# A two-dimensional spectral filter on one core: three quarters of stage 1's constants loaded without their zeros, its matmuls writing every fourth place of PSUM

## The chip, the cores and the metric

The kernel runs on one core of a Trainium2 chip. The metric is the time of one execution on the device in microseconds (us), as a median of several runs. A core has five engines with instruction streams of their own: TensorE (PE, matmuls; PEld is its weight load), VectorE (DVE), ScalarE (ACT), GpSimd (POOL) and SyncE (SP, which here only issues transfers). They meet through semaphores. Matmuls read SBUF and write PSUM, which has eight banks of 512 fp32 per partition.

## The reference

```python
def _A_ref(x, w_r, w_i):
    B, S, D = x.shape
    X = jnp.fft.rfft2(x.astype(jnp.float32), axes=(-2, -1))
    W = w_r + 1j * w_i
    X = X * W
    y = jnp.fft.irfft2(X, s=(S, D), axes=(-2, -1)).astype(jnp.bfloat16)
    return y
...
x = A_x
g = _sigmoid((x * gate_w).sum(-1, keepdims=True))
a = _A_ref(x, A_w_r, A_w_i)
b = _B_ref(x, B_w_r, B_w_i)      # the same filter with other weights
return g * a + (1 - g) * b
```

x is 1 x 2048 x 1024 in bf16, and each weight is 2048 x 513 (real and imaginary part, for A and B). So one picture is transformed, its spectrum is multiplied with two complex masks, both products are transformed back, and a gate per row mixes the two.

## The kernel before

All transforms are matmuls with constant matrices, and a 2048-point transform is split in two steps of 32 and 64 points. Stage 1 does the 32-point step over the rows, stage 2 the transform over the columns, stage 4 the 64-point step. Then VectorE multiplies with the masks (`product`, L508), and stages 5 to 7 go back: `group` (L604 matmuls, L615 copies), `stage6` (L754) and `stage7` (L783 matmuls, L790 and L794 results).

Each engine runs its instructions in the order in which the program adds them; `Prog` puts waits where a key that one instruction reads or writes was touched by another. A DMA is in the stream of the engine that issues it and can hold up what stands behind it there.

Stage 1 works on four blocks of rows, c = 0 to 3. A block holds four residues r = 4c + q, and a partition is n1 * 4 + b, with n1 of 32 and b of 4. For a block:

- SP loads x (nine loads for the four blocks, 4 MB in all), and VectorE folds it into `XF` (`fold`, L340), twice over, as sums and as differences (h).
- The constants of stage 1 are in the tile `MM`: four blocks of 512 columns, one block for each c, and behind them, from column 2048, the same negated (`negate`, L359 on ScalarE for blocks 0 and 1, L357 on VectorE for 2 and 3). Column r * 128 + t * 8 + ri * 4 + b' of `MM` belongs to residue r, frequency t, real or imaginary part ri, and row class b'. On partition n1 * 4 + b it is other than zero only where b' = b: three quarters of `MM` are zeros.
- 32 matmuls (L379) have 128 x 128 of `XF` as weights and stream 256 columns: 128 of `MM` twice, once as they are and once negated (or twice as they are). Two matmuls add up in one stretch of 256 fp32 of PSUM. Eight of them fill two banks (a slot u of four), and one copy of 1024 elements per partition (L390 on ScalarE, L388 on VectorE for two of the sixteen) takes them to `FT`.

The order of the matmuls is block by block; inside a block by h, then by the half j, then by residue q. A matmul waits for its fold, for its constants and for their negation.

The constants come in three loads: block 0 from ScalarE's queue, ahead of its table load, its sigmoid and its negation; block 1 from SP behind the three x loads of block 0; blocks 2 and 3 in one load from SP behind the two x loads of block 1. SP goes on with the rest of x, the constants of stage 2 (`F2`), the gate's weights (`GR`), `CK`, `SM` and then the 44 loads of the masks into `W` (`wload`), which VectorE's products wait for. VectorE's stream begins with the folds of blocks 0 and 1. `fold3` (L438) and `stage2` (L451, L460) follow stage 1 and read `FT`.

Outputs of matmuls in the other stages lie in PSUM in runs of 32 and more, with two small exceptions: `star_column` (L527) writes 15 columns to every second place, and some matmuls of two columns write 32 places apart. `col0` (L582) reads its moving operand from `W` with a step of one row of 520 elements, or from `XF` side by side.

Of the kernel before, what the change touches and what calls it, by code (L numbers as in the profile page):

```python
# [17 lines left out]
def bf16_bits(a):  # L18
    a = np.ascontiguousarray(np.asarray(a, dtype=np.float32))
    u = a.view(np.uint32).astype(np.uint64)  # L20
    r = ((u + 0x7FFF + ((u >> 16) & 1)) >> 16).astype(np.uint16)
    return r


def make_consts():
    C = {}
    pi2 = 2 * np.pi
    n1 = np.arange(32)
    M = np.zeros((32, 4, 16, 16, 2, 4))
    V = np.zeros((2, 4, 16, 32, 16))  # L30
    for b in range(4):
        for r in range(16):
            n2 = 16 * b + r
            for t in range(16):
# [5 lines left out]
                else:  # L40
# [2 lines left out]
                    M[:, b, r, t, 1, b] = -np.sin(ph)  # L43
                    V[0, b, r, :, t] = np.cos(ph) / 16
                    V[1, b, r, :, t] = -np.sin(ph) / 16
    C["M"] = M.reshape(128, 2048)
    VR = 0.25 * V.reshape(128, 512)
    row = np.arange(128)
    MK = np.zeros((128, 16, 4))
# [4 lines left out]
    for cmb, par in ((0, 0), (1, 1), (2, 1), (3, 0)):  # L54
# [5 lines left out]
        else:  # L60
            F = F[0].reshape(128, 2, 2, 32, 2)
            e = [np.stack([F[:, :, 0, :, w], F[:, :, 1, :, 1 - w]], axis=2).reshape(128, 128) for w in range(2)]
# [28 lines left out]
    c, s = np.cos(pi2 * kk * o2 / 64), np.sin(pi2 * kk * o2 / 64)  # L91
# [4 lines left out]
    e = np.eye(64)  # L96
# [12 lines left out]
    sl_, f = row % 32, row // 32 % 2  # L109
# [14 lines left out]
    for pi in range(2):  # L124
        for h in range(2):
# [5 lines left out]
            a = pi2 * l * (d + 0.5) / 1024  # L131
# [100 lines left out]

def bass_gated_mix__spectral_gfnet__spectral_gfnet__prompt_kernel(nc, A_x, A_w_r, A_w_i, B_x, B_w_r, B_w_i, gate_w, out):
    C = make_consts()
    SMv = C.pop("SM")
    cst = {k: nc.inline_tensor(bf16_bits(v), name=f"c_{k}") for k, v in C.items()}
    cst_sm = nc.inline_tensor(np.ascontiguousarray(SMv, dtype=np.float32), name="c_SM")
    f32, u16 = dt.float32, dt.uint16
# [5 lines left out]
    MM = sb("MM", 7168)  # L244
# [13 lines left out]
    def sl(t, off, dims, p0=0, np_=128, pstep=1):  # L258
        n = t.shape[1]
        return AP(t, p0 * n + off, [[n * pstep, np_]] + [list(x) for x in dims])  # L260

    def ps(col, dims):
        return AP(PS, col, [[4096, 128]] + [list(x) for x in dims])

    def bank(b):
        return ("ps", b)
# [9 lines left out]
    P = Prog()  # L276
# [5 lines left out]
    def dma(eng, name, dst, src, **kw):  # L282
        return P.add(eng, lambda e: e.dma_start(dst, src), dma=name, **kw)  # L283

    def load(name, tile, off, n, src, eng="sp", **kw):
        dma(eng, name, sl(tile, off, [(1, n)]).bitcast(u16), src, **kw)


    def xloc(c):
        return W, (96 + 8 * c) * RP  # L290
# [4 lines left out]
    for _ in range(18):  # L295
        P.add("pe", lambda e: e.matmul(ps(7 * 512, [(1, 256)]), sl(CL, GRo, [(1, 128)]), sl(CL, GRo, [(1, 256)]), start=True, stop=True),
              r=["GRz"], w=[bank(7)])
    def mload(eng, c0, n):
        load(f"M{c0}", MM, c0 * 512, n * 512, cst["M"].ap()[:, c0 * 512:(c0 + n) * 512], eng=eng, w=[("M", c) for c in range(c0, c0 + n)])

    mload("act", 0, 1)
    for c in range(4):
        t, o = xloc(c)
        for q0, n in XPARTS[c]:
            dma("sp", f"x{c}{q0}", sl(t, o + q0 * 1024, [(1, n * 1024)]), xv[:, (4 * c + q0) * 1024:(4 * c + q0 + n) * 1024], w=[("x", c, q0)])
        if c < 2:
            mload("sp", 1 + c, 1 + c)
    load("F2", F2, 0, 1536, cst["F2"].ap(), w=["F2"])
    dma("sp", "GR", sl(CL, GRo, [(1, 128)], np_=8), AP(gate_w.tensor, gate_w.offset, [[128, 8], [1, 128]]), w=["GRz"], a=["GR"])
    load("CK", CK, 0, 1056, cst["CK"].ap(), w=["CK", "GW2"])  # L310
# [40 lines left out]
            fold(c, q0, n, h)  # L351

    def negate(c, n=1, eng="act"):
        dst, src = sl(MM, 2048 + c * 512, [(1, n * 512)]), sl(MM, c * 512, [(1, n * 512)])
        kw = dict(r=[("M", k) for k in range(c, c + n)], w=[("NM", k) for k in range(c, c + n)])
        if eng == "dve":
            P.add("dve", lambda e: e.tensor_scalar(out=dst, in0=src, scalar1=-1.0, scalar2=None, op0=ALU.mult), **kw)  # L357
        else:
            P.add("act", lambda e: e.activation(dst, src, ACT.Copy, scale=-1.0), **kw)  # L359
# [3 lines left out]
    def stage1(c):  # L363
        nonlocal cnt
        us = [(cnt + k) % 4 for k in range(4)]
        cnt += 4
        parts = XPARTS[c] if c == 0 else ((0, 4),)
        for q0, n in parts:
            for h in range(2):
                for j in range(2):  # L370
                    u = us[2 * h + j]
                    for q in range(q0, q0 + n):
                        r = 4 * c + q
                        base = (c % 2) * 4096 + q * 1024 + h * 512
                        o = ps(u * 1024 + q * 256, [(1, 256)])
                        for s in range(2):
                            lh = sl(XF, base + 256 * s + 128 * j, [(1, 128)])
                            rh = sl(MM, r * 128, [(2048 * s, 2), (1, 128)])
                            P.add("pe", lambda e, o=o, lh=lh, rh=rh, s=s: e.matmul(o, lh, rh, start=(s == 0), stop=(s == 1)),  # L379
                                  r=[("xf", c % 2, q, h, s ^ j), ("M", c), ("NM", c)], w=[bank(2 * u + q // 2)])  # L380
                    if q0 + n < 4:
                        continue
                    for m0, mn in ((0, 32), (32, 96)) if (c, h, j) == (3, 1, 1) else ((0, 128),):
                        src = ps(u * 1024 + m0, [(128, 2), (1, mn), (256, 4)])
                        dst = sl(FT, h * 8192 + j * 2048 + 16 * m0 + 4 * c, [(4096, 2), (16, mn), (1, 4)])
                        kw = dict(r=[bank(2 * u), bank(2 * u + 1)], a=[("F1", h, j)] + [("F1a", h, j)] * (m0 == 0))
                        if (c, h, j) in ((2, 1, 1), (3, 0, 1)):
                            P.add("dve", lambda e, s=src, d=dst: e.tensor_copy(d, s), **kw)  # L388
                        else:
                            P.add("act", lambda e, s=src, d=dst: e.activation(d, s, ACT.Copy), **kw)  # L390

    negate(0)
    negate(1)
    folds(0)
    folds(1)
    negate(2, 2, "dve")
    stage1(0)
    stage1(1)
    fold(2, 0, 2, 0)
    fold(2, 2, 2, 0)  # L400
    fold(2, 0, 4, 1)
    folds(3)
    stage1(2)
    stage1(3)

# [276 lines left out]
    def spare():  # L682
        slots.append(slots.pop(0))
        return slots[-1]
# [33 lines left out]
    u = spare()  # L718
# [207 lines left out]
```

## Time and profile before

| | |
|---|---|
| median of 3 runs | 118.17 us (118.08 to 118.53) |
| profiled execution | 118.88 us, span 116.6 us |
| PE, PEld busy | 110.0 us (94%), 88.4 us (76%) |
| DVE, ACT, POOL busy | 100.7 us (86%), 96.5 us (83%), 34.0 us (29%) |
| granted TensorE clock | 0.991 |
| DMA | 26.14 MB, 17682 packets, mean 224 GB/s |
| stage-1 matmuls (L379) | 128, 14.9 us, 273 ns each |
| their weight loads | 128, 12.2 us, 98 ns each |
| copies L390 | 15, 13.1 us, 1012 ns each |
| folds L340 | 34, 11.4 us, 5.9 us idle before them |
| first load of M, on ACT | 128 KB, 3.7 us from issue to landing |

Times are those of one profiled execution; starts count from its span's start, and about 2.3 us of the execution lie around the span. The time of an instruction reaches from its start to its end; matmuls overlap, so that the distance from one start to the next (the pitch) is shorter than the time of one. A group's line has its busy time, the mean of one in ns, and the idle time of its engine just before.

### The profile page before, as it was taken

What the parts mean: (1) busy time and instruction counts of PE and PEld (TensorE: products, weight loads), DVE (VectorE), ACT (ScalarE), POOL (GpSimd) and SP (SyncE); (2) the same over time, 40 slices, a digit from 0 to 9 for tenths busy, and PEclk for the clock granted to TensorE, in tenths of its full rate; (3) what the DMA queues carried; (4) which work ended last, traced back from release to release, by engine and by line L of the source; (5) the groups of instructions that cost most, each with busy time, mean ns of one, the idle gap of its engine ahead of it and who ended that gap; (6) DMA issues with size and microseconds to landing.
All of it is one profiled execution on the core that took longest, in us unless ns stands there. A gap on an engine that the chain in (4) does not pass through costs nothing.

```text
span 116.6 us, 4237 instructions
## 1 busy us (share of the span) xinstructions
PE 110.0 (94%) x1812; PEld 88.4 (76%) x1812; DVE 100.7 (86%) x210; ACT 96.5 (83%) x117; POOL 34.0 (29%) x43
## 2 busy tenths in 40 slices
PE   6999999999999999999999999999999999999950
PEld 4666888875766657569999999999988777777430
DVE  0478998978999999699999999999568999899990
ACT  5239998997799999939999999997879889988420
POOL 1000030016655600000000000000002999999930
PEclk9999999999999999999999999999999999999996
DMA  3999999999999999962369930000000135425466
GB/s 86 289 405 415 421 359 355 352 349 350 363 370 358 368 364 362 350 241 100 139 172 407 389 123 0 6 0 6 0 6 0 46 146 181 181 96 193 153 233 236
DMA packets 17682, 26.14 MB, mean 224 GB/s; under 512 B 2112, under 2 KB 11072, under 8 KB 17664
## 3 DMA queue, kind: packets, MB, share of 16 engines
q1 hardware_dynamic: 16368, 23.00, 56.2%
q0 software_dynamic: 864, 2.36, 5.6%
q10 hardware_dynamic: 432, 0.52, 1.4%
q8 instruction: 14, 0.23, 0.8%
q14 instruction: 4, 0.03, 0.1%
HBM read 17.48 MB, written 4.19 MB: 186 GB/s over the span
## 4 chain that ended last, share of the span: by engine, by line
PE 51%; SPq 29%; DMA 9%; DVE 3%; issue 2%; ACT 2%; DVEq 0%
SPq L283 29%; PE PS L604 26%; PE PS L783 15%; PE PS L754 7%; DMA W<-in_B_w_i_dram 6%; DMA W<-in_A_x_dram 3%; PE PS L379 2%; DVE W L508 1%; DVE MM L794 1%; ACT W L615 1%; PE PS L563 1%; ACT XF L790 1%; PE PS L582 1%; DVE XF L340 0%; DVEq L865 0%
## 5 line engine op out<-in xcount | busy, mean ns | idle before, releaser
L604 PE MATMUL PS<-CL,W 128*128 128x128 bf16 x512 | 32.3, 225 | 0.2 <-DVE W L508 0.2
L604 PEld LDWEIGHTS PS<-CL,W 128*128 128x128 bf16 x512 | 31.6, 145 | 0.9 <-DVE W L508 0.7
L835 POOL TENSOR_TENSOR MM<-FT 128x512 bf16<-128x512 f32 x14 | 17.4, 1273 | 48.7 <-DVE FT L830 48.7
L615 ACT ACTIVATE W<-PS 128x1024 bf16<-128x1024 f32 (+1 forms) x30 | 28.5, 1036 | 3.0 <-PE PS L604 2.9
L508 DVE TENSOR_TENSOR W<-XF,W 128x1024 bf16<-128x1024 bf16 (+1 forms) x38 | 22.4, 608 | 1.6 <-DMA W<-in_B_w_i_dram 0.9
L508 DVE TENSOR_TENSOR W<-MM,W 128x1024 bf16<-128x1024 bf16 (+1 forms) x38 | 22.4, 613 | 0.2
L783 PE MATMUL PS<-FT,W 128*128 128x256 bf16 (+1 forms) x132 | 19.4, 299 | 0.1
L487 ACT ACTIVATE XF<-PS 128x1024 bf16<-128x1024 f32 x16 | 17.3, 1079 | 1.6 <-PE PS L480 1.6
L480 PE MATMUL PS<-XF,CK 128*128 128x512 bf16 (+1 forms) x72 | 17.8, 357 | 0.1
L767 ACT ACTIVATE W<-PS 128x1024 bf16<-128x1024 f32 (+1 forms) x15 | 14.8, 992 | 2.7 <-PE PS L754 2.7
L340 DVE TENSOR_TENSOR XF<-W 128x512 bf16<-128x512 bf16 (+2 forms) x34 | 11.4, 404 | 5.9 <-DMA W<-in_A_x_dram 5.7
L783 PEld LDWEIGHTS PS<-FT,W 128*128 128x128 bf16 x132 | 12.1, 98 | 5.4 <-DVE XF L794 0.7
L379 PE MATMUL PS<-MM,XF 128*128 128x256 bf16 x128 | 14.9, 273 | 0.6 <-DVE XF L340 0.4
L469 ACT ACTIVATE XF<-PS 128x1024 bf16<-128x1024 f32 x14 | 15.0, 1078 | 0.1
L379 PEld LDWEIGHTS PS<-MM,XF 128*128 128x128 bf16 x128 | 12.2, 98 | 3.5 <-DVE XF L340 2.0
L390 ACT ACTIVATE FT<-PS 128x1024 bf16<-128x1024 f32 (+2 forms) x15 | 13.1, 1012 | 0.8 <-PE PS L379 0.8
L283 POOL DMA_DIRECT2D MM<-XF x18 | 9.9, 550 | 13.4 <-PE PS L480 8.0
L830 DVE TENSOR_TENSOR FT<-PS,XF 128x512 f32<-128x512 f32 x18 | 11.6, 684 | 0.8 <-ACT XF L790 0.4
L451 PEld LDWEIGHTS PS<-F,FT 128*128 128x128 bf16 x128 | 8.4, 98 | 3.1 <-ACT FT L390 0.2
L790 ACT ACTIVATE XF<-PS 128x512 f32<-128x512 f32 (+1 forms) x16 | 8.5, 533 | 2.2 <-PE PS L783 2.2
L451 PE MATMUL PS<-F,FT 128*128 128x128 bf16 x128 | 10.2, 219 | 0.0
L480 PEld LDWEIGHTS PS<-XF,CK 128*128 128x128 bf16 x72 | 4.7, 97 | 6.1 <-ACT XF L487 5.7
(62 smaller groups left out, 104.3 us busy)
## 6 DMA issues: line engine op xcount, KB each, us to landing
W<-in_A_x_dram SPq DMA_DIRECT2D x7, 512.0 KB, 7.5
out_dram<-MM SPq DMA_DIRECT2D x10, 256.0 KB, 2.5
MM<-XF POOLq DMA_DIRECT2D x18, 128.0 KB, 5.4
FT<-c_U SPq DMA_DIRECT2D x1, 2048.0 KB, 8.5
MM<-XF SPq DMA_DIRECT2D x14, 128.0 KB, 2.7
W<-in_A_w_r_dram SPq DMA_DIRECT2D x4, 256.5 KB, 6.3
W<-in_A_w_i_dram SPq DMA_DIRECT2D x4, 256.5 KB, 6.7
W<-in_B_w_r_dram SPq DMA_DIRECT2D x4, 256.5 KB, 7.1
```

What stands on the lines that cost most here:

```text
L283: return P.add(eng, lambda e: e.dma_start(dst, src), dma=name, **kw)
L379: P.add("pe", lambda e, o=o, lh=lh, rh=rh, s=s: e.matmul(o, lh, rh, start=(s == 0), stop=(s == 1)), r=[("xf", c % 2, q, h, s ^ j), ("M", c ...
L451: P.add("pe", lambda e, o=o, cs=cs, j=j, t=t, rh=rh: e.matmul(o, fblock(1 + cs, j, t), rh, start=(j == 0), stop=(j == 1)), r=[("F1a" if p ...
L469: P.add("act", lambda e: e.activation(dst, src, ACT.Copy), **kw)
L480: P.add("pe", lambda e, o=o, kind=kind, pm=pm, m=m, rh=rh: e.matmul(o, sl(CK, fbo(kind, pm, m), [(1, 128)]), rh, start=(m == 0), stop=(m = ...
L487: P.add("act", lambda e: e.activation(dst, src, ACT.Copy), **kw)
L508: P.add("dve", lambda e: e.tensor_tensor(out=rows((1 - h) * 64 * RP + sw * HW), in0=sl(xt, xo + 128 * h + 64 * h0, [(0, 2), (256, 4 * ni), ...
L604: P.add("pe", lambda e, o=o, l0=l0, ab=ab: e.matmul(o, sl(W, HW * ab + l0, [(RP, 128)]), sl(CL, KIo[ab], [(1, 128)]), start=(ab == 0), sto ...
L615: P.add("act", lambda e: e.activation(dst, src, ACT.Copy), r=b, a=keys)
L767: P.add("act", lambda e, s=src, d=dst: e.activation(d, s, ACT.Copy), **kw)
L783: P.add("pe", lambda e: e.matmul(ps(col, [(1, n * 256)]), lh, rh, start=(k == 0), stop=(k == last)), r=[("Y", r), "DI"] + ["DJ"] * (full o ...
L835: P.add("pool", lambda e, s=s, op=op: e.tensor_tensor(out=ods(s, 0, 2), in0=pv[:, :, 0, :], in1=pv[:, :, 1, :], op=op), r=[("PQ", pk, 0), ...
```

## The change

The constants of block 0 are loaded as before, 128 KB, with their columns in another order: by b' first. Of blocks 1 to 3 only the quarter that isn't zero is kept in memory, 384 columns by 128 rows. VectorE clears columns 512 to 2047 of `MM`, and four loads of 32 rows by 384 columns (24 KB each, 768 bytes a row), two from ScalarE's queue and two from SP's, put the rows of each class b in every fourth partition and in that class's 384 columns. They wait for the clearing and share one semaphore. The negations of blocks 1 to 3 read and write four runs of 128 or 256 columns each. A stage-1 matmul reads its 128 columns of `MM` as four runs of 32, and since PSUM is to hold what it held before, writes column b', k to place 4 k + b'. Counts of matmuls, folds and copies stay, and nothing after stage 1 is touched.

```diff
-    C["M"] = M.reshape(128, 2048)
+    MF = M[:, :, :4].transpose(0, 1, 5, 2, 3, 4).reshape(128, 512)
+    MC = np.stack([M[:, b, 4:, :, :, b] for b in range(4)]).reshape(128, 384)
+    C["M"] = np.concatenate([MF, MC], axis=1)
...
-    def mload(eng, c0, n):
-        load(f"M{c0}", MM, c0 * 512, n * 512, cst["M"].ap()[:, c0 * 512:(c0 + n) * 512], eng=eng, w=[("M", c) for c in range(c0, c0 + n)])
-
-    mload("act", 0, 1)
+    load("M0", MM, 0, 512, cst["M"].ap()[:, :512], eng="act", w=[("M", 0)])
+    MR = [("M", c) for c in range(1, 4)]
+    mz = P.add("dve", lambda e: e.memset(sl(MM, 512, [(1, 1536)]), 0.0), w=MR)
+
+    def mrest(eng, gs):
+        for g in gs:
+            dma(eng, "M1", sl(MM, 512 + 384 * g, [(1, 384)], p0=g, np_=32, pstep=4).bitcast(u16), cst["M"].ap()[32 * g:32 * g + 32, 512:],
+                a=MR, after=[mz])
+
+    mrest("act", (0, 1))
     for c in range(4):
         t, o = xloc(c)
         for q0, n in XPARTS[c]:
             dma("sp", f"x{c}{q0}", sl(t, o + q0 * 1024, [(1, n * 1024)]), xv[:, (4 * c + q0) * 1024:(4 * c + q0 + n) * 1024], w=[("x", c, q0)])
-        if c < 2:
-            mload("sp", 1 + c, 1 + c)
+        if c == 0:
+            mrest("sp", (2, 3))
...
     def negate(c, n=1, eng="act"):
-        dst, src = sl(MM, 2048 + c * 512, [(1, n * 512)]), sl(MM, c * 512, [(1, n * 512)])
+        dst, src = (sl(MM, o + (384 + c * 128 if c else 0), [(384 if c else 128, 4), (1, n * 128)]) for o in (2048, 0))
...
-                        o = ps(u * 1024 + q * 256, [(1, 256)])
+                        o = ps(u * 1024 + q * 256, [(128, 2), (1, 4), (4, 32)])
                         for s in range(2):
                             lh = sl(XF, base + 256 * s + 128 * j, [(1, 128)])
-                            rh = sl(MM, r * 128, [(2048 * s, 2), (1, 128)])
+                            rh = sl(MM, r * 32 + 384 * (c > 0), [(2048 * s, 2), (384 if c else 128, 4), (1, 32)])
```

## The prediction

> **What bounds the kernel now.** I read the page first, then the busy time by stage, then the timeline of TensorE and VectorE, then the waits. The chain of waits on the page is led by "SPq L283 29%", the issuing of loads. I do not take that as the bound of the first stage: the chain's last link in that stretch is a W transfer, and the timeline shows what that link is worth.
>
> ```profile
> 5.20:20.40 15.20, 14.66 (x128) 12.24 (x129) 13.61 (x36) 12.35 (x14) 1.31 (x1) 1.00 1.03 391
> 20.40:49.50 29.10, 28.95 (x443) 19.60 (x441) 26.84 (x56) 27.37 (x33) 9.87 (x18) 1.00 1.07 359
> ```
>
> These are the windows: length, then busy time of PE, weight loads, DVE, ACT and POOL, the granted clock, the DMA share and GB/s. The first is stage 1. All its 128 matmuls lie in it, PE is busy 14.66 of 15.20 us at full clock, and DMA moves 391 GB/s.
>
> ```profile
> 5.24 1.91 PE L379 MATMUL PS<-MM,XF 128*128 128x256 bf16 x16
> 13.80 6.82 PE L379 MATMUL PS<-MM,XF 128*128 128x256 bf16 x61
> 20.46 0.20 PE L516 MATMUL PS<-CK,CL 128*128 128x8 bf16 x2
> 48.18 0.44 DVE L508 TENSOR_TENSOR W<-MM,W 128x512 bf16<-128x512 bf16 x1
> 49.51 0.42 DVE L508 TENSOR_TENSOR W<-XF,W 128x512 bf16<-128x512 bf16 x1 [0.89 <-DMA W<-in_B_w_i_dram]
> ```
>
> In the timeline (start, length, engine) the 61 matmuls take 6.82 us. One lasts 0.273, so the pitch is (6.82 - 0.27)/60 = 0.109 us. From 10.5 us on PE runs without a gap to the end of stage 1 at 20.46. TensorE is the bound there; before it, folds that wait for x cost it gaps of together some 1.3 us (15.22 from start to end, less 128 x 0.109). From 33 to 48.6 us VectorE's products and ScalarE's evacuations (one of L469 or L487 every 0.91 us) run without gaps. The W transfers that head the chain then hold VectorE up for 0.89 us, once. From 53.5 to 85 TensorE is full again (17.47 of 17.5 us, then 14.00 of 14.0). Nearly every later step therefore hangs on the end of stage 1, with 0.89 us of slack in between.
>
> **The change, part by part.** Times are those of the profiled execution, 118.88 us with a span of 116.6, which is 0.71 over the median of 118.17. I add differences to both alike.
>
> *Fewer bytes.* Two loads go, 128 KB and 256 KB on SP. Four of 24 KB come: 288 KB less. At the 391 GB/s of the window that is 0.75 us less transfer. SP loses issues of 0.43 and 0.56 us and gains two; the smallest issues on the page's timeline (2 KB) cost 0.35, so SP is 0.1 to 0.3 us earlier. What this can buy is the 0.89 us that VectorE waits for W, and no more, since it waits for no other W load.
>
> *The clearing of the tile.* One VectorE MEMSET of 768 words, ahead of its first fold at 4.64, before which it is idle. POOL's MEMSET of 256 elements took 0.31, so three times as many come to some 0.9 us, done by 1.7. Bounds: 0.3 to 1.2 (a VectorE copy of 1024 elements), and all of them end before 2.2.
>
> *Two issues on ScalarE, behind that wait.* They stand ahead of its table load (1.28 us), its sigmoid (0.20) and the negation of the first block. M0's issue there took 0.36. So 1.7 + 0.72 + 1.28 + 0.20 = 3.9 us; M0 landed at 4.44 and the negation started at 4.46. The cover is 0.5 us, and what exceeds it would delay the first matmul one to one. I take nothing. Queued behind SP's wait are the x loads of blocks 1 to 3, but SP arrives there at 2.1, after the MEMSET.
>
> *The negations read and write runs of 128.* The folds write runs of 128 too, so I take 0.63 and 0.42 us as they are. M1 lands as late as before at worst (7.2 us), and block 1 begins only after 32 matmuls: no cost, with two us to spare.
>
> *The matmuls.* Same count, 256 columns, same weights. Their moving operand comes in runs of 32. Their output goes to every fourth fp32 of PSUM. The page of before has no such output; the nearest rows, by shape:
>
> ```profile
> L379 PE MATMUL PS<-MM,XF 128*128 128x256 bf16 x128 | 14.9, 273 | 0.6 <-DVE XF L340 0.4
> L527 PE MATMUL PS<-GSB,CK 128*128 128x15 bf16 x2 | 0.2, 176 | 0.0
> L527 PE MATMUL PS<-GSB,CK 128*128 128x1 bf16 x2 | 0.2, 164 | 0.0
> L582 PE MATMUL PS<-XF,CL 128*128 128x64 bf16 x2 | 0.4, 188 | 0.0
> L582 PE MATMUL PS<-XF,CL 128*128 128x60 bf16 x2 | 0.4, 188 | 0.0
> L582 PE MATMUL PS<-W,CL 128*128 128x64 bf16 x2 | 0.6, 276 | 0.0
> ```
>
> The fourth number is ns of one. A contiguous output costs (273 - 188)/(256 - 64) = 0.44 ns per column. L527 writes 15 columns to every second place of PSUM (its output is `[(2, n)]`): (176 - 164)/14 = 0.86 ns per column, twice as much. It also reads its operand at step 2, but L582's 60 columns from XF are read at steps of 2 and -1 and written contiguously, and cost the same 188 ns as 64 contiguous ones. So a small step in the read is free, and I put L527's excess down to the write. The excess is 6 ns on two rows, each rounded to 1 ns: a hint, not a measurement. The runs of 32 in the read I take as free by the same L582 row.
>
> Bounds for a step of four: below, nothing, as ScalarE reads PSUM at a step of 256 (L390, 1023 ns per 1024 elements) as fast as contiguously (L487, 1023), though at under half of TensorE's rate (0.91 us per 1024 elements from copy to copy, against 0.109 per 256). Above, the price of a read with each element far from the next: L582 from W, 276 against 188, is 88/64 = 1.4 ns more per column. I take L527's factor of two, the only row with a stepped PSUM write: a pitch of 2 x 0.109 = 0.218 us.
>
> The Trainium skill, page "PSUM — Partial Sum Buffer", section Specifications (TRN2), says that PSUM is laid out in 8-byte lines and that any non-contiguous pattern slows matmuls significantly. It gives no factor; a step of two fp32 already puts each element in a line of its own, so by that rule L527's price would hold for a step of four. L527 is the only row here that agrees, by its 6 ns.
>
> *The sum.* Stage 1 starts at 5.24 as before and is then bound by TensorE alone: 128 x 0.218 = 27.9 us, an end at 33.1 in place of 20.46, so 12.7 later (the 1.3 us of old gaps are swallowed; without them it would be 14.0). PSUM evacuation has room: eight matmuls now take 1.74 us against 0.91 for the ScalarE copy that follows. The folds of blocks 2 and 3 get more time. Late next are the sums and differences of L438 on VectorE, the second stage and the products, all of them hung on stage 1's end. W lands by 49 us while its last user comes at 61, so the 0.89 us wait goes. 12.7 - 0.9 = **11.8 us**: 130.7 for the profiled execution, 130.0 against the median. Own range of this case 128.5 (a shorter tail of evacuations and swaps that land sooner in a quiet DMA) to 131.5 (0.86 ns per column, no gain at W).
>
> **Rivals.** *Stepped PSUM writes run at full rate* (not slower). Then stage 1's end stays near 20.4, because x for block 1 is still queued behind 96 KB of M and the gap at 10 us remains. The gain is W landing 0.75 us sooner, in place of 0.89 us of waiting: 117.4, or 118.2 if SP's issue rate holds W back rather than bandwidth. It decides as long as the pitch stays under 0.116 (0.9/128 above 0.109). For it: ScalarE's free stepped reads, and that L527's evidence is 6 ns. Against it: that this is still the only row with stepped writes, and it doubles. Chance 0.16, with 0.09 for a gain over 0.6 us and 0.07 within it.
>
> *Each write pays as each scattered read does.* L582 from W: 1.4 ns more per column, 256 columns, 128 matmuls: 45 us, so about 162. For it: step four goes further than step two. Against it: L527's step two already leaves no two elements side by side, and costs 0.43 more. Chance 0.08. The Trainium skill, page "SBUF — State Buffer", section "Door 1: The DMA port swizzle", lets each access to a new 16-byte line pay a penalty in SBUF; L582 from W agrees there with its 88 ns, and no row shows PSUM doing so.
>
> *A part of the penalty hides in the array's pipeline*, leaving a pitch of about 0.150: 128 x 0.041 = 5.2 us, less 1.3 of gaps and 0.9 at W: 121 to 123. Nothing in the page speaks for it but the smallness of the hint. Chance 0.06.
>
> **How the numbers follow.** Forecast 0.70, rivals 0.16, 0.08 and 0.06. The time is the forecast's. The range from 117.4 to 131.5 takes in the full-rate case, the partial case and the forecast, and leaves out the scattered price (0.08) and a tenth of the forecast's own spread. What can be told from no change here is 0.5%, 0.6 us: faster 0.09, same 0.07, slower 0.84.
>
> **What would show it.** Right: the stage-1 matmul lasts some 380 ns where it lasted 273, a run of n of them takes 0.217 to 0.222 us each, ScalarE waits some 0.8 us for TensorE ahead of each stage-1 copy, the first product starts near 37.5 in place of 25.2, VectorE's wait for in_B_w_i is gone, and the stretch after stage 5's start has its old length. Wrong: a row that still says 273 ns and a pitch of 0.109 means the full-rate case; 600 ns and more the scattered price; a first matmul later than 5.4 us means that the clearing or ScalarE's queue was not covered.

## The result, and the profile after

The changed kernel takes 130.44 us (median of 6 runs, 130.38 to 131.09) against 118.47 us for the kernel before (median of 6): a ratio of 1.103, with a 95% interval of 1.100 to 1.106. The profiled execution took 131.09 us with a span of 128.8, and 118.88 with 116.6 before.

The timeline of TensorE in the changed kernel (start, length, engine, line, count; stage 1's matmuls are now L387):

```profile
5.04 28.46 PE L387 MATMUL PS<-MM,XF 128*128 128x256 bf16 x128
33.29 0.24 PE L524 MATMUL PS<-CK,CL 128*128 128x8 bf16 x2
```

One unbroken stretch of 128 matmuls replaces 15.2 us with gaps. What follows it starts at 33.29 in place of 20.46, 12.83 us later. The groups by shape (busy time, mean ns of one, then the idle time before them and what ended it) and the busy time by stage (PE, weight loads, DVE, ACT, POOL, clock, DMA share, GB/s):

```profile
L387 PE MATMUL PS<-MM,XF 128*128 128x256 bf16 x128 | 28.5, 428 | 0.0
L387 PEld LDWEIGHTS PS<-MM,XF 128*128 128x128 bf16 x128 | 17.9, 141 | 10.4 <-issue 0.6 <-DVE XF L348 0.4
L398 ACT ACTIVATE FT<-PS 128x1024 bf16<-128x1024 f32 x13 | 13.0, 1025 | 11.4 <-PE PS L387 11.4
```

```profile
5.20:20.40 15.20, 15.20 (x69) 9.64 (x68) 10.85 (x31) 8.15 (x9) 0.53 (x1) 1.00 1.01 374
20.40:33.20 12.80, 12.80 (x61) 8.27 (x60) 3.43 (x7) 5.46 (x6) 0.00 (x0) 1.00 1.10 349
33.20:61.50 28.30, 28.15 (x430) 19.12 (x428) 26.17 (x53) 26.23 (x31) 9.88 (x18) 1.00 0.66 220
```

In the first 15.2 us only 69 matmuls fit where 128 did, and ScalarE, which began 13 copies in that window, begins 8; through stage 1 it waits 11.4 us for TensorE. The third window is the second stage and the products. They take as long as before and are only moved: from the first matmul behind stage 1 to the first of stage 5 (L612, at 63.56 us; 50.80 before) it is 30.27 us, where it was 30.34. The DMA share fell from 1.07 to 0.66, since the last piece of W now lands at 43.9 us (49.4 before), well inside this window. VectorE's wait for W is gone; in the waits from 32 us on, no transfer is listed. The chain of waits says the same in one line each, which in the page of before began with "SPq 29%":

```profile
PE 92%; ACT 3%; DVE 1%; issue 0%; DVEq 0%; POOL 0%; POOLq 0%
PE PS L612 24%; PE PS L387 22%; PE PS L791 13%; PE PS L488 11%; PE PS L762 7%; PE PS L459 5%; PE PS L298 3%; PE PS L468 3%; PE PS L530 2%; ACT XF L495 2%; DVE MM L802 1%; PE PS L571 1%; ACT XF L477 1%; ACT XF L798 1%; PE PS L590 1%
```

### The profile page after: what moved, and what is told of

It is laid out like the page before. It is cut to its first block, busy times and chain, and to the rows that moved or that the text cites. A ratio compares the mean times of both kernels' runs of the same rounds, so it can differ in the third digit from the quotient of the medians.

```text
span 128.8 us, 4241 instructions
## 1 busy us (share of the span) xinstructions
PE 123.0 (96%) x1812; PEld 94.2 (73%) x1812; DVE 101.8 (79%) x211; ACT 97.3 (76%) x117; POOL 33.2 (26%) x43
## 4 chain that ended last, share of the span: by engine, by line
PE 92%; ACT 3%; DVE 1%; issue 0%; DVEq 0%; POOL 0%; POOLq 0%
PE PS L612 24%; PE PS L387 22%; PE PS L791 13%; PE PS L488 11%; PE PS L762 7%; PE PS L459 5%; PE PS L298 3%; PE PS L468 3%; PE PS L530 2%; ACT XF L495 2%; DVE MM L802 1%; PE PS L571 1%; ACT XF L477 1%; ACT XF L798 1%; PE PS L590 1%
## 5 line engine op out<-in xcount | busy, mean ns | idle before, releaser
L612 PE MATMUL PS<-CL,W 128*128 128x128 bf16 x512 | 31.9, 224 | 0.0
L612 PEld LDWEIGHTS PS<-CL,W 128*128 128x128 bf16 x512 | 31.6, 145 | 0.3
L387 PE MATMUL PS<-MM,XF 128*128 128x256 bf16 x128 | 28.5, 428 | 0.0
L387 PEld LDWEIGHTS PS<-MM,XF 128*128 128x128 bf16 x128 | 17.9, 141 | 10.4 <-issue 0.6
L398 ACT ACTIVATE FT<-PS 128x1024 bf16<-128x1024 f32 (+2 forms) x15 | 14.1, 968 | 12.1 <-PE PS L387 11.4
L495 ACT ACTIVATE XF<-PS 128x1024 bf16<-128x1024 f32 x16 | 17.3, 1079 | 1.6 <-PE PS L488 1.6
L791 PEld LDWEIGHTS PS<-FT,W 128*128 128x128 bf16 x132 | 12.1, 98 | 5.4 <-DVE XF L802 0.7
```

The costliest lines, as they stand in the source:

```text
L495: P.add("act", lambda e: e.activation(dst, src, ACT.Copy), **kw)
L612: P.add("pe", lambda e, o=o, l0=l0, ab=ab: e.matmul(o, sl(W, HW * ab + l0, [(RP, 128)]), sl(CL, KIo[ab], [(1, 128)]), start=(ab == 0), sto ...
L791: P.add("pe", lambda e: e.matmul(ps(col, [(1, n * 256)]), lh, rh, start=(k == 0), stop=(k == last)), r=[("Y", r), "DI"] + ["DJ"] * (full o ...
```

## The experiments

The theory is that a matmul that writes PSUM at a step pays for the write. The rivals are that it pays for reading its moving operand in runs of 32, and, once the write is blamed, that the cost grows with the distance or with the number of jumps. The kernels of `e1_read` to `e6_half` compute something else than the reference, since they write stage 1's columns to other places than the stages behind it read; the matmuls keep their number and, but for `e5_step3`, their size.

### The write or the read: `e1_read` and `e2_write4`

`e1_read` is the changed kernel with the old places:

```diff
-                        o = ps(u * 1024 + q * 256, [(128, 2), (1, 4), (4, 32)])
+                        o = ps(u * 1024 + q * 256, [(1, 256)])
```

> The changed kernel, but its stage-1 matmuls write 256 places side by side; the read in four runs of 32 and the smaller loads stay. The spectrum then comes out in another order, so the output is not the reference's. If the stepped write is the cause (theory): pitch 0.109 us, 273 ns each, stage 1 ends near 20.4, and what is left is the worth of the smaller loads, 117.4 to 118.5 us. If the read in runs of 32 is the cause (rival): pitch 0.216, 130.4 us.

`e2_write4` is the kernel before with that line turned round.

> The kernel before, with nothing changed but the places that stage 1 writes: every fourth, as in the changed kernel. Its constants are in the old order, so the output is not the reference's. Theory (the write): pitch 0.216 us, 128 x 0.107 = 13.7 more on TensorE, less 1.3 of gaps that it swallows and less the 0.89 us wait for W: 130.0. Rival (the read): 118.5, pitch 0.109.

Timelines of TensorE, `e1_read` first (with the group of its matmuls by shape), then `e2_write4`:

```profile
L387 PE MATMUL PS<-MM,XF 128*128 128x256 bf16 x128 | 14.9, 273 | 0.6 <-DVE XF L348 0.5
5.04 1.94 PE L387 MATMUL PS<-MM,XF 128*128 128x256 bf16 x16
7.48 13.11 PE L387 MATMUL PS<-MM,XF 128*128 128x256 bf16 x112 [0.50 <-DVE XF L348]
```

```profile
5.00 27.79 PE L379 MATMUL PS<-MM,XF 128*128 128x256 bf16 x128
```

With the old places and the new read, the matmuls are as they were (273 ns each; the first 16 start (1.94 - 0.27)/15 = 0.111 us apart; stage 1 is over at 20.6 us) and the time is 118.26 us, a ratio of 0.9995 (0.997 to 1.002) to the kernel before. With the new places and the old loads the 128 matmuls last 27.79 us. One of them takes 0.421, so the pitch is (27.79 - 0.42)/127 = 0.216 us; the time is 131.16 us, ratio 1.109 (1.106 to 1.111). The write alone makes the whole difference, and the read costs nothing that can be measured. `e2_write4` is 1.2 us above the 130.0 that was expected. There 0.9 had been taken off for the wait for W; the section on W says why it did not come back, and the last section what else lengthens some executions. `e1_read` also measures what the change was left to gain with a free write: nothing that can be measured.

### What a stepped write costs: `e3_write2`, `e4_pairs`, `e5_step3`

All three are the kernel before with other places for the 256 columns. (`e5_step3` has 255 of them, which it reads side by side, and its 18 warm-up matmuls, which run ahead of stage 1, write all banks once.)

```diff
-                        o = ps(u * 1024 + q * 256, [(1, 256)])
+                        o = ps(u * 1024 + q * 256, [(128, 2), (1, 2), (2, 64)])     # e3_write2
+                        o = ps(u * 1024 + q * 256, [(2, 2), (4, 64), (1, 2)])       # e4_pairs
+                        o = ps(u * 1024 + q * 256, [(1, 3), (3, 85)])               # e5_step3
```

> As e2, but every second place is written (two interleaved runs of 64 for each 128 columns). If two neighbours in PSUM share one write and all else costs a write each (theory), a step of two costs what a step of four does: pitch 0.216 us, 130 us. If the cost grows with the distance (rival), the pitch lies between, 0.15 to 0.18, and the time at 122 to 126. If small steps are free: 118.5.

> As e2, but written in runs of two places, one run in every four places, twice. If neighbouring pairs are the unit (theory): pitch 0.109 us, 118.5 us. If every jump costs (rival): half as many jumps, pitch 0.16, 124 us; if any pattern other than a long run halves the rate: 0.216, 130 us.

> The kernel before, with stage-1 outputs of 255 columns at a step of three, so that odd and even places alternate; the values are not the reference's, and the warm-up matmuls, as many as before, write all banks once. If two neighbours share one write and all else costs a write each (theory): 0.215 us pitch, 130 us. If the limit were two halves of PSUM, one of odd and one of even places (rival): 0.109, 118.4 us.

Their stage-1 groups by shape, in that order:

```profile
L379 PE MATMUL PS<-MM,XF 128*128 128x256 bf16 x128 | 28.3, 426 | 0.0
```

```profile
L379 PE MATMUL PS<-MM,XF 128*128 128x256 bf16 x128 | 14.8, 273 | 0.8 <-DVE XF L340 0.7
```

```profile
L379 PE MATMUL PS<-MM,XF 128*128 128x255 bf16 x128 | 28.1, 424 | 0.6 <-DVE XF L340 0.6
```

A step of two costs what a step of four does (131.09 us in its one execution), and so does a step of three (131.55 in one), which refutes the rival that PSUM has two halves, one of odd and one of even places, each with a limit of its own: at a step of three odd and even places alternate. Runs of two at every fourth place, each starting at an even one, cost nothing in the matmul: 273 ns, as side by side. The distance does not matter and jumps as such do not; what matters is whether two columns that follow each other go to two neighbouring places. (That all places are filled in the end, as in the changed kernel and in `e3_write2`, does not help.) Whether such a pair has to start at an even place, and what runs of three would cost, no run here shows. The Trainium skill, page "PSUM — Partial Sum Buffer", section Specifications (TRN2), gives PSUM lines of 8 bytes, which is two fp32, and this fits. The Trainium skill also says there that any non-contiguous pattern slows matmuls significantly. Here the slowdown is a factor of two (0.216 against 0.109 us for 256 columns), and the pairs, which are not contiguous, lose nothing, so that these words give way to the measurement.

The one execution of `e4_pairs` took 119.59 us, 1.2 more than the kernel before. Its stage 1 is no longer than before, and its trace has 1.1 us of waiting elsewhere, at L555, which reads a small transfer (XST) that landed at 60.4 us, where it was 58.7 in the trace of the kernel before; the section on W takes that up.

### Does all of it reach the end: `e6_half`

```diff
-                        o = ps(u * 1024 + q * 256, [(1, 256)])
+                        o = ps(u * 1024 + q * 256, [(128, 2), (1, 4), (4, 32)] if c > 1 else [(1, 256)])
```

> The kernel before, with the step of four in the writes of blocks 2 and 3 alone, 64 of 128 matmuls (output not the reference's). Theory: every ns goes through to the end but for the 0.89 us wait for W: 64 x 0.107 = 6.8, less 0.9: 124.4 us. Rival (a stretch of slack after stage 1 takes a share of it): under 123.5.

It took 125.33 us against 118.54 on the same chip, ratio 1.056 (1.053 to 1.058). That is 6.79 us for 64 x 0.107 = 6.85. By these medians all of it reaches the end, and the 0.9 us that should have come back did not. The rival, that slack swallows a share, has nothing for it either.

### The wait for W: `b2` and `e8_more`

`b2` is the kernel before, unchanged. `e8_more` loads 512 KB of constants once more (stage 2's copies wait for that load too, but it lands at 16.8 us, ahead of them):

```diff
         if c < 2:
             mload("sp", 1 + c, 1 + c)
+    again = dma("sp", "MX", sl(MM, 4096, [(1, 2048)]).bitcast(u16), cst["M"].ap())
...
-    last1 = [P.ops["pe"][-1]]
+    last1 = [P.ops["pe"][-1], again]
```

> The kernel before, unchanged, profiled a second time, to see whether VectorE's wait for W is a trait of the kernel or of the one execution shown. If it is a trait: 0.9 us of waiting for W near 49.5, the span near 116.6. If it is one of that execution: less than 0.4 us, as in the run with pairs, whose loads are the same, and the stretch from the first product to stage 5 shorter by some 0.5.

> The kernel before with 512 KB of constants loaded once more, unused, on SP's queue behind the loads of block 1: 1.3 us of transfer at 391 GB/s, more than the change took away. If W bounds the middle of the kernel with no slack (the 0.89 us wait is a trait): 1.3 later, 119.8. If W has about half a us of slack in most executions, as the nil effect of smaller loads suggests: 0.4 to 0.9 later, 119.0 to 119.4. If x for block 1, queued behind it or not, decides: no more than 118.8.

The waits between 20 and 66 us (engine and line, for what: us in total, times, longest), of `b2`, then of `e8_more`:

```profile
DVE XF L555 <- DMA XST<-XST: 1.5, 1, 1.5
```

```profile
DVE W L509 <- DMA W<-in_B_w_i_dram: 2.2, 2, 1.1
DVE XF L556 <- DMA XST<-XST: 1.3, 1, 1.3
```

In this second execution of the same kernel, on another chip, VectorE waits for no W at all (its last piece landed at 48.84 us, not 49.42); it waits 1.5 us for a small transfer, the exchange of the special column (XST), which it did not wait for in the first, and its span is 117.8. In `e4_pairs`, whose loads are the same, the wait for W is 0.3 us. So the 0.89 us is no trait of the kernel: it differs from execution to execution.

More bytes do cost: 120.87 us against 119.31 on that chip, ratio 1.013 (1.007 to 1.018). These 1.6 us (0.8 to 2.2) are about the 1.3 us of their transfer, as the first of the three cases had it, but not for its reason, since the wait that it called a trait is none. They cost it at other places than the one I had in view: at 26 and 33 us, where the first pieces of W are late. The W loads sit at the edge: later ones are felt here, and earlier ones were not in `e1_read`, which loads 288 KB less. Why the XST exchange is slow in some executions stays open.

### A version with the old writes: `e7_spread`

```diff
+    load("M0", MM, 0, 512, cst["M"].ap()[:, :512], eng="act", w=[("M", 0)])
+    load("MC", MM, 4096, 388, cst["M"].ap()[:, 512:], eng="act", w=["MC"])
...
+    def spread(c, n):
+        P.add("pool", lambda e: e.tensor_tensor(out=sl(MM, c * 512, [(4, n * 128), (1, 4)]), in0=sl(MM, 3972 + c * 128, [(1, n * 128), (0, 4)]),
+                                                in1=sl(MM, 4096, [(0, n * 128), (1, 4)]), op=ALU.mult), r=["MC"], w=[("M", k) for k in range(c, c + n)])
+
+    spread(1, 1)
+    spread(2, 2)
```

> The whole computation, with the old writes side by side: the constants of blocks 1 to 3 come without their zeros in one load of 97 KB on ScalarE's queue, and GpSimd spreads them to the old order by a product with a mask of 0 and 1 (two instructions, 512 and 1024 elements). Theory: W lands up to 0.7 us sooner, its 0.89 us wait shrinks by as much, pitch 0.109: 117.7 us. Rival (the spread is late, 1.3 and 2.5 us on GpSimd behind the load, and block 1 or 2 waits for it): 118.5 to 119.5.

119.42 us, ratio 1.010 (1.006 to 1.014): worse than the kernel before, and for neither reason. Two views of it, the timeline of GpSimd and TensorE and the groups between 5 and 8 us on VectorE:

```profile
4.88 2.94 POOL L306 TENSOR_TENSOR MM<-MM 128x512 bf16<-128x512 bf16 x2 [3.79 <-DMA MM<-c_M]
8.02 5.21 PE L382 MATMUL PS<-MM,XF 128*128 128x256 bf16 x43 [1.23 <-DVE XF L343]
```

```profile
L343 DVE TENSOR_TENSOR XF<-W 128x256 bf16<-128x256 bf16 x3 | 3.0, 1046 | 0.2 <-DMA W<-in_A_x_dram 0.2
```

The spread is done in time. But beside GpSimd's two products, two of VectorE's folds of 256 elements take 0.89 and 1.98 us, where they take 0.285 in the kernel before. They end at 6.06 and 7.96 us, each 0.15 behind the end of a product (5.91 and 7.81), and the fold behind them takes 0.28 again; 1046 ns is the mean of these three. TensorE waits 1.23 us for them, and stage 1 ends 1.25 us later. The Trainium skill, page "SBUF — State Buffer", section "Who interferes with whom", has it that a VectorE instruction with two SBUF inputs contends with a GpSimd instruction that reads SBUF. The trace agrees: both folds last until a product is over. A spread on another engine was not tried: `e1_read` bounds what any such version could gain, and that is nothing measurable. No run beats the kernel before.

## Why the prediction was right, point by point

- **The pitch.** Twice 0.109 was forecast, 0.218; it is 0.216. The hint in L527, 6 ns on two rows, was real, and the step of its read was rightly acquitted: `e3_write2` steps in the write alone and has the same price. The row's own price, 0.86 ns per column, is 0.216/256 = 0.84 in the pitch.
- **The duration of one row** was forecast at 380 ns and is 421 (428 in the mean). Start to start, a matmul costs 107 ns more, but start to end it shows 148 more, and its weight load 141 in place of 98. Sums from pitches hold; sums from durations would have been 38% too high (148 ns for 107).
- **Stage 1's end** was forecast 12.7 later; it is 12.83. That it is so near is in part luck. It started 0.2 earlier, its matmuls take 128 x 0.216 = 27.65 in place of 27.9, and 0.6 more is lost at its start (last section), which the forecast did not have. In `e2_write4`, which lost nearly nothing there, the next stage starts at 32.58, 12.1 later.
- **What comes back.** Of 12.83 us, 12.2 reach the end of the profiled execution, so 0.6 came back where 0.9 was forecast. This is the term that was mis-sized, and that it is no further off is luck. From the first matmul behind stage 1 to the end of the span it is 96.1 us in the trace of before and 95.5 in the changed kernel; in `e1_read`, `e2_write4` and `e6_half`, where VectorE waits for no W either, it is 95.6 to 95.7. So, by this comparison, the wait of 0.89 cost the end 0.5 to 0.6 even in the execution that has it. In `b2` it does not exist, and by its medians `e6_half` gave nothing back. The profile of one execution showed a wait that came last there, not one that always does. By medians the difference is 11.97 us, where 11.8 was forecast, and the time is 130.44, where 130.0 was. The stretch from stage 5's first matmul on was to keep its length; it is 65.3 us where it was 65.8, and here most of the wait for W comes back.
- **The clearing** was given 0.9 us and took 0.70, done at 1.67.
- **SP's two issues** took 0.52 and 0.59, so that SP reached the load of `F2` at 6.45, 0.02 earlier than before and not 0.1 to 0.3.
- **ScalarE's two issues** took 0.51 and 0.61 in place of 0.36 each. That used up the cover of 0.5: the sigmoid began at 4.17 and the negation at 4.28, 0.3 us after its constants had landed (3.96). This did delay the first matmul, though by little. The view puts the weight load's wait of 0.36 us down to a fold, but the two folds that the first two matmuls read had ended at 4.65, and the negation ended at 4.89: in ten of the eleven traces the first weight load of stage 1 starts 0.11 us behind the end of the negation. In `e7_spread`, whose negation ends at 4.54, stage 1 starts at 4.92, right behind the warm-up matmuls. So at most 0.12 of the 0.3 us reached the first matmul, at 5.04, where the prediction took nothing. Stage 1 still starts 0.2 earlier than before, because its first constants landed at 3.96 in place of 4.44. Four lines of the changed kernel, then two of the kernel before (the fourth and the last are the weight loads):

```profile
0.97 0.70 DVE L302 MEMSET MM<- 128x768 uint32 x1 [0.97 <-PEq L919]
4.17 0.20 ACT L319 ACTIVATE DUM<-DUM 128x1 f32<-128x1 f32 x1
4.28 0.61 ACT L367 ACTIVATE MM<-MM 128x512 bf16<-128x512 bf16 x1
5.01 0.14 PEld L387 LDWEIGHTS PS<-MM,XF 128*128 128x128 bf16 x2 [0.36 <-DVE XF L348]
```

```profile
4.46 0.63 ACT L359 ACTIVATE MM<-MM 128x512 bf16<-128x512 bf16 x1 [1.84 <-DMA MM<-c_M]
5.21 1.66 PEld L379 LDWEIGHTS PS<-MM,XF 128*128 128x128 bf16 x16 [0.57 <-DVE XF L340]
```

- **ScalarE's waits** of some 0.8 us ahead of each copy are 0.70, and 2.43 where VectorE takes the copy between; the first product starts at 38.0 (37.5 forecast).
- **The full-rate rival** was priced at 117.4, or 118.2 if W was not held by bandwidth. `e1_read` is that rival, and 118.26, where the kernel before takes 118.42 on that chip, says that its gain was not there to be had. The reads of ScalarE that spoke for it were given as 1023 ns for both patterns; by shape they are 1075 (L390) and 1079 (L487), still alike. **The scattered price and the partly hidden one** are refuted by the pitch.

## What to carry to other kernels

A reordering that saves a little transfer is paid for in full if it moves a step into a matmul's output in a stage that TensorE bounds: ask first whether the columns, in the order in which they are streamed, go to neighbouring places of PSUM at least two by two, and if not, count the columns twice. Runs of two that start at even places are enough. A wait that the trace of one execution shows is a price only after a second execution shows it too, and two small rows of the right kind (here a matmul with 15 columns) are worth more than a large row of the wrong kind.

## What was not expected of the hardware

Stage 1 sometimes begins at half the matmul rate. The window of these two answers is the same 1.6 us, in the changed kernel and in `e2_write4` (PE busy and, in brackets, matmuls):

```profile
5.00:6.60 1.60, 1.60 (x6) 0.90 (x6) 0.86 (x5) 0.00 (x0) 0.00 (x0) 1.00 1.01 386
```

```profile
5.00:6.60 1.60, 1.60 (x9) 1.06 (x9) 1.11 (x6) 0.00 (x0) 0.00 (x0) 1.00 1.02 357
```

With the last warm-up matmul, which both counts take in, nine run in the one where six do in the other. In the trace of the changed kernel the first three distances from start to start are 0.295, 0.427 and 0.427 us, and 0.216 from the fifth on. That costs 0.6 us, which is the distance between the spans of these two executions (128.8 and 128.2). In `e7_spread`, with contiguous writes, the first distances are 0.213 where later ones are 0.109. The clock column reads 1.00 in both answers, so it does not show it. The 18 warm-up matmuls, which start at 1.1 us, are 0.213 apart too in every trace, but for the last four in `e8_more`, which are 0.109 to 0.113 apart. So the rate doubles at another time in each execution: by the starts, some 2.8 us behind the first warm-up matmul in `e8_more` and some 5.3 in the changed kernel.

The Trainium skill, page "TensorE: Matmul & The Clock Gate", Part 1, tells of a clock at half rate until a window of some 3.4 us of activity has passed, at a phase that varies from run to run. The halved rate and the varying time fit; the 3.4 us lies between the two times above. Such a start is not the change's doing, since it shows with contiguous writes too; its 0.6 us are half a per cent of the time. Of the six executions of the changed kernel, two have spans of 128.7 and 128.8 us and four of 128.2, and four of the five of `e2_write4` are 0.6 to 0.9 us longer than the one with the trace; that the longer ones began like this would fit, but is not shown, as each kernel has one trace.
